# Attention and two expert layers on one core: queries held 128 tokens at a time in place of 64

## The chip, the cores and the metric

The kernel runs on one core of a Trainium2 chip. The metric is the device time of one execution in microseconds, the median over several runs. In the rows of the profile PE is the matrix engine (TensorE), PEld its weight loads, DVE the vector engine, ACT the scalar engine, POOL the GpSimd engine; SP issues most DMAs.

## What is computed

```python
# attention without softmax: 8 batches, 8 heads, 576 tokens, head size 64
kv  = np.einsum('bhsd,bhse->bhde', k, v)          # 64x64 for each batch and head
out = np.einsum('bhsd,bhde->bhse', q, kv)         # the product that is changed here
rms = np.sqrt(np.mean(out * out, axis=-1, keepdims=True) + 1e-06)
x   = out / rms * g_norm                          # then laid out as 4608 tokens x 512
# dense layer, 512 -> 768 -> 512
h = np.maximum(np.maximum(x @ w1, x @ w2), x @ w3)
x = h @ w_out
# 8 experts, 512 -> 1024 -> 512, two for each token
noisy_logits = x @ w_gate + np.log1p(np.exp(x @ w_noise)) * noise
# the two largest, a softmax over the two, and
# out[token] += weight * (relu(x @ w1[e]) @ w2[e])
```

All in fp32; the kernel gets the accuracy of the large layers with pairs of fp32r tiles (a high and a low part, three products).

## The kernel before

The 4608 tokens go through the first part in nine chunks of 512 (`NCH`, `CT`). For each chunk the kernel makes the attention output of its tokens (`ao`), norms it (`norm_a` to `norm_c`: a square on ACT, a sum for each head on DVE, a root, a scaling), turns it so that features lie on partitions (`xtrans` on TensorE in the first two chunks, `planes_out` and a transposing DMA later), multiplies it by the dense layer's 18 column groups (`g1`, L353) and back (`g2`, L399), routes the tokens (`route_a`, `route_b`) and scatters their rows to a table in DRAM. After the last chunk comes the expert stage (`unit`, with L1180, L1194 and L1242 as its matmuls), from 676 us on, which takes the larger part of the time.

`ao(c, j, banks)` makes half a chunk: two blocks `i` of 128 tokens. The keys' and values' product of a batch lies in a tile `KB` of 128 partitions x 256: two heads stand on top of each other (partitions 0 to 63 and 64 to 127, `HALF`), and the four pairs `p` of heads side by side. The queries lie in the same way, features on partitions and tokens along the row. In each call the queries are what TensorE holds (its weights) and 64 columns of `KB` what streams through. The result has tokens on partitions: head half `h` goes to bank `h`, and pair `p` and block `i` choose the columns in it. There are two banks for each half chunk, with 16 calls in each block.

A batch is 576 tokens, four and a half blocks. So at tokens 576, 1728, 2880 and 4032 the border of two batches lies in the middle of a block, and the two halves of that block need different tiles `KB`.

The order on TensorE is as the code is written, apart from the first chunk: there `run_tasks` places tasks by costs that are written beside them (`ao0`, the first half of chunk 1, is one of these, with cost 1.0, and `ao1`, the second half, is another). From chunk 2 on `attend` calls `ao` for the next chunk at the twelfth column group of `g1`, both halves one after the other, between two matmul groups of the dense layer. The tiles' results are read by the squares at once (L230), and by `norm_c` (L250) later in the same chunk.

Other matmuls in plain fp32 that are named below: L187 multiplies keys by values, with weights of 128 x 64 (two heads in two column halves) and, for the last 64 tokens of a batch, of 64 x 64; L561 is a part of the gate's weights' preparation, with weights of 128 x 128 and 16 streaming columns; L543 and L272 are transposes; L457 and L458 have 16-bit weights.

Of the kernel before, what the change touches and what calls it, by code (L numbers as in the profile page):

```python
# [18 lines left out]
NB, NH, S, D = 8, 8, 576, 64  # L19
T, DM, DF, NE, DE = 4608, 512, 768, 8, 1024  # L20
NCH, CT = 9, 512
# [61 lines left out]
def body(tc, A, dbg=None):  # L83
    nc = tc.nc
    PE, ACT, DVE, POOL, SP = nc.tensor, nc.scalar, nc.vector, nc.gpsimd, nc.sync
# [19 lines left out]
    KB = [sb1.tile([128, 256], F, name=f"kvt{i}") for i in range(2)]  # L105
# [59 lines left out]
    def qv(c):  # L165
        return qbuf[c][:, 0:2048].rearrange("p (a t) -> p a t", a=4)
# [9 lines left out]
    HALF = [slice(0, 64), slice(64, 128)]  # L176
# [25 lines left out]
    def ao(c, j, banks):  # L202
        for h in range(2):
            ao_bank[c, 2 * j + h] = banks[h]
        for i in range(2):
            t0 = (2 * j + i) * 128
            for p in range(4):
                o = slice(i * 256 + p * 64, i * 256 + (p + 1) * 64)
                for x in range(2):
                    t = t0 + x * 64  # L210
                    kb = KB[(c * CT + t) // S % 2]
                    for h in range(2):
                        PE.matmul(banks[h][HALF[x], o], qv(c)[HALF[h], p, t:t + 64],
                                  kb[HALF[h], p * 64:(p + 1) * 64], start=True, stop=True)

    xn_of = {}
    xn_n = [0]
# [98 lines left out]
    def attend(c, n):  # L316
        if n == 0:
            for j in range(2):
                ao(c, j, [abank(), abank()])
        if n < 2:  # L320
            for b in (2 * n, 2 * n + 1):
                norm_a(c, b)
        if n == 1:
            norm_b1(c, 0, 4)
            norm_b2(c, 0, 4)
        if n in (2, 3):
            j = n - 2
            for b in (2 * j, 2 * j + 1):
                norm_c(c, b)
                planes_out(c, b)  # L330
            planes_turn(c, j)
# [280 lines left out]
    for j in range(2):  # L612
        ao(0, j, [abank(), abank()])
        for i in range(2):
            norm_a(0, 2 * j + i)
# [123 lines left out]
    for i in range(2):  # L739
        if i == 0:  # L740
            task("ao0", "PE", 1.0, ["q1", "kvo", "x0l3", "ev0"] + done, lambda: ao(1, 0, [abank(), abank()]), 0)
        task(f"n1s{i}", "ACT", 0.6, ["ao0", "t03"], lambda i=i: norm_sq(1, i, x1[i]), 0.6)
        task(f"n1r{i}", "DVE", 0.69, [f"n1s{i}"], lambda i=i: norm_red(1, i), 0.6)
# [261 lines left out]
    c = NCH - 1  # L1005
# [444 lines left out]
```

## Time and profile before

| | us |
|---|---|
| median of 3 runs | 1505.43 (1503.96 to 1508.12) |
| the profiled execution | 1503.61 |
| its span in the trace | 1501.8 |
| TensorE matmuls busy | 1476.2 (98%) |
| TensorE weight loads busy | 1260.4 (84%) |
| VectorE busy | 749.5 (50%) |
| ScalarE busy | 644.2 (43%) |

The profile is of one execution. The span begins with the first recorded instruction and ends with the last; the execution's own time is 1.8 us longer. Busy time is the union of an engine's instructions; matmuls are pipelined, and a matmul's length in the rows is from its start to its modelled end, so that many can lie over each other. The same is true of weight loads: a load's length tells how long one takes, and the distance between the starts of two tells their pace.

### The profile page before, as it was taken

To read this page: it belongs to the slowest core of one execution; us is meant where nothing else is said; L and a number is where in the kernel's file an instruction comes from. 1 tells how busy PE (TensorE), PEld (TensorE's weight loads), DVE (VectorE), ACT (ScalarE), POOL (GpSimd) and SP (SyncE) were. 2 spreads that over 40 slices of the span, in tenths; PEclk is the share of its full clock that TensorE was granted. 3 is DMA by queue.
4 is the path that set the end of the run, shared out by engine and by line. 5 is a ranking of instruction groups with operands and counts; after the bars stand their busy time and mean duration, and the time that the engine had idled before them with its cause. 6 is when DMAs were issued, how large, how long until landed. Compare 5 with 4: busy or idle time off the path is not lost.

```text
span 1501.8 us, 22899 instructions
## 1 busy us (share of the span) xinstructions
PE 1476.2 (98%) x9190; PEld 1260.4 (84%) x9190; DVE 749.5 (50%) x1513; ACT 644.2 (43%) x1020; POOL 223.3 (15%) x332
## 2 busy tenths in 40 slices
PE   6999999999999999999999999999999999999997
PEld 6889989898989888888888878887888888888886
DVE  6985545454444444458344454553454374444443
ACT  4653524242424233334444454544454364444443
POOL 0000111102020202023211102202211111110112
PEclk9999999999999999999999999999999999999999
DMA  7412435142332303083776668767565587554555
GB/s 315 144 70 99 152 117 149 72 149 86 126 114 99 121 29 122 0 240 107 200 200 140 173 217 227 194 186 199 135 162 137 147 216 196 132 135 140 139 121 108
DMA packets 160724, 218.43 MB, mean 145 GB/s; under 512 B 124320, under 2 KB 124704, under 8 KB 145120
## 3 DMA queue, kind: packets, MB, share of 16 engines
q1 hardware_dynamic: 140624, 165.14, 35.0%
q0 software_dynamic: 19984, 51.73, 15.1%
q8 instruction: 74, 1.21, 0.3%
q14 instruction: 42, 0.34, 0.1%
HBM read 137.86 MB, written 51.72 MB: 126 GB/s over the span
## 4 chain that ended last, share of the span: by engine, by line
PE 54%; POOL 0%; issue 0%; ACT 0%; POOLq 0%
PE bank L1242 26%; PE bank L1180 26%; PE bank L1194 1%; PE bank L1283 1%; PE bank L1298 0%; PE bank L399 0%; POOL out L1216 0%; PE bank L1205 0%; ACT W L334 0%; PE bank L1289 0%; ACT xn L1247 0%; POOLq L1398 0%; ACT RA L406 0%; PE bank L1136 0%; POOL spacer L1215 0%
## 5 line engine op out<-in xcount | busy, mean ns | idle before, releaser
L353 PE MATMUL bank<-B,W 128*128 128x512 f32 (+1 forms) x2184 | 453.1, 367 | 2.2 <-ACT W L532 2.1
L353 PEld LDWEIGHTS bank<-B,W 128*128 128x128 f32 x2184 | 376.4, 188 | 70.4 <-ACT W L532 2.5
L1242 PE MATMUL bank<-W,B 128*128 128x512 f32 x1704 | 411.2, 390 | 0.0
L1242 PEld LDWEIGHTS bank<-W,B 128*128 128x128 f32 x1704 | 318.6, 188 | 64.5
L1180 PE MATMUL bank<-B,W 128*128 128x512 f32 (+4 forms) x1536 | 361.0, 374 | 0.0
L1180 PEld LDWEIGHTS bank<-B,W 128*128 128x128 f32 x1536 | 278.1, 188 | 53.7 <-issue 4.4
L335 DVE TENSOR_TENSOR W<-G,W 128x1024 fp32r<-128x1024 f32 x168 | 203.0, 1224 | 121.8 <-ACT W L334 121.3
L1184 ACT ACTIVATE B<-bank 128x512 fp32r<-128x512 f32 (+4 forms) x152 | 85.8, 565 | 334.3 <-PE bank L1180 334.3
L1185 DVE SCALAR_TENSOR_TENSOR B<-bank,B 128x512 fp32r<-128x512 f32 (+4 forms) x152 | 98.7, 649 | 249.0 <-ACT B L1184 248.4
L334 ACT ACTIVATE W<-G 128x1024 fp32r<-128x1024 f32 x168 | 175.4, 1055 | 43.5 <-PE bank L1242 24.9
L399 PE MATMUL bank<-W,B 128*128 128x256 f32 (+1 forms) x1296 | 161.0, 284 | 0.4 <-DVE B L361 0.2
L399 PEld LDWEIGHTS bank<-W,B 128*128 128x128 f32 x1296 | 159.5, 188 | 1.6 <-ACT RA L406 0.5
L472 POOL DMA_INDIRECT Xg<-RA,si x72 | 70.7, 981 | 582.0 <-issue 403.7
L371 DVE TENSOR_TENSOR hm<-hm,bank 128x512 f32<-128x512 f32 (+1 forms) x107 | 69.6, 651 | 115.2 <-PE bank L353 109.8
L1216 POOL DMA_INDIRECT out<-xn,idt x36 | 59.2, 1644 | 402.9 <-ACT xn L1247 397.6
L357 ACT ACTIVATE B<-hm 128x512 fp32r<-128x512 f32 (+1 forms) x53 | 32.2, 607 | 172.4 <-DVE hm L371 172.4
L1180 PE MATMUL bank<-xlo,W 128*128 128x512 f32 (+2 forms) x288 | 73.3, 376 | 0.0
L1180 PEld LDWEIGHTS bank<-xlo,W 128*128 128x128 f32 x288 | 52.5, 188 | 9.8
L369 ACT ACTIVATE hm<-bank 128x512 f32<-128x512 f32 (+1 forms) x54 | 30.4, 564 | 64.1 <-PE bank L353 52.2
L406 ACT COPY RA<-bank 128x256 uint16<-128x256 uint16 x72 | 25.6, 372 | 68.6 <-DVE RA L406 63.2
L1216 POOL DMA_INDIRECT out<-hm,idt x20 | 31.9, 1593 | 131.2 <-ACT hm L1247 127.4
L361 DVE TENSOR_TENSOR B<-hm,B 128x512 fp32r<-128x512 f32 (+1 forms) x53 | 35.1, 661 | 32.2 <-ACT B L357 32.2
(230 smaller groups left out, 1034.8 us busy)
## 6 DMA issues: line engine op xcount, KB each, us to landing
G<-mw SPq DMA_DIRECT2D x84, 1024.0 KB, 5.1
G<-w1s SPq DMA_DIRECT2D x12, 1024.0 KB, 4.9
kv<-kv SPq DMA_DIRECT2D x8, 1024.0 KB, 7.1
G<-kv SPq DMA_DIRECT2D x8, 1024.0 KB, 9.2
RB<-qT SPq DMA_DIRECT2D x8, 1024.0 KB, 4.9
G<-mw SPq DMA_DIRECT2D x16, 512.0 KB, 6.4
out<-pad POOLq DMA_DIRECT2D x5, 1280.0 KB, 6.5
out<-pad POOLq DMA_DIRECT2D x2, 1536.0 KB, 6.7
```

Source lines behind the costliest of these rows:

```text
L334: ACT.activation(w[:, 0:1024], src, AF.Copy)
L335: DVE.tensor_tensor(w[:, 1024:2048], src, w[:, 0:1024].bitcast(F), op=OP.subtract)
L353: PE.matmul(bank[:, 0:t1 - t0], w_in(g)[:, a, k, s], x[b][:, k, t0:t1], start=n == 0 and k == 0, stop=n == 2 and k == 3)
L361: DVE.tensor_tensor(h[:, 1], hm, h[:, 0].bitcast(F), op=OP.subtract)
L371: DVE.tensor_tensor(hm, hm, bank, op=OP.max)
L399: PE.matmul(x2b[i][z][:, 0:hi - lo], h[:, a, s], w[:, b, lo:hi], start=f == 0 and n == 0, stop=f == 5 and n == 2)
L472: i = POOL.indirect_dma_start(out=Xg, out_offset=bass.IndirectOffsetOnAxis(ap=idx, axis=0), in_=src, in_offset=None)
L1180: PE.matmul(bank[:, 0:n], w[:, a, k, s], x[b][:, k, 0:n], start=z == 0, stop=z == 11)
L1184: ACT.activation(h[:, 0, 0:n], bank[:, 0:n], AF.Relu)
L1185: DVE.scalar_tensor_tensor(h[:, 1, 0:n], bank[:, 0:n], 0.0, h[:, 0, 0:n].bitcast(F), op0=OP.max, op1=OP.subtract)
L1216: d = POOL.indirect_dma_start(out=A["out"], out_offset=bass.IndirectOffsetOnAxis(ap=idt[u % 3][:, i:i + 1], axis=0), in_=y, in_offset=None ...
L1242: PE.matmul(obank[i], h[:, a, s], w[:, b, ff % 2, :], start=ff == 0 and n == 0, stop=ff == 7 and n == 2)
```

## The change

A block of 128 tokens that lies in one batch is no longer cut in two. Its queries are held by TensorE as 64 x 128 tiles (64 features of a head, 128 tokens), one for each head half, where there were four of 64 x 64. A block on the border of two batches is cut as before.

```diff
             t0 = (2 * j + i) * 128
             for p in range(4):
                 o = slice(i * 256 + p * 64, i * 256 + (p + 1) * 64)
-                for x in range(2):
-                    t = t0 + x * 64
-                    kb = KB[(c * CT + t) // S % 2]
+                k = [KB[(c * CT + t) // S % 2] for t in (t0, t0 + 64)]
+                w = 128 if k[0] is k[1] else 64
+                for x in range(0, 128, w):
                     for h in range(2):
-                        PE.matmul(banks[h][HALF[x], o], qv(c)[HALF[h], p, t:t + 64],
-                                  kb[HALF[h], p * 64:(p + 1) * 64], start=True, stop=True)
+                        PE.matmul(banks[h][x:x + w, o], qv(c)[HALF[h], p, t0 + x:t0 + x + w],
+                                  k[x // 64][HALF[h], p * 64:(p + 1) * 64], start=True, stop=True)
```

TensorE's instructions where chunk 2's product begins, before the change; a row is a call, the last figures are the partitions and columns of what it writes, `bank6` and `bank7` take the two head halves, `kvt0` and `kvt1` are the two tiles `KB`, and RB has the queries:

```order
L353 MATMUL bank3_108<-B0_85,W5_75 128x256 x12
L353 MATMUL bank0_105<-B0_85,W5_75 128x256 x12
L213 MATMUL bank6_111<-kvt1_91,RB_89 64x64
L213 MATMUL bank7_112<-kvt1_91,RB_89 64x64
L213 MATMUL bank6_111<-kvt1_91,RB_89 64x64
L213 MATMUL bank7_112<-kvt1_91,RB_89 64x64
```

And the same place in the changed kernel:

```order
L353 MATMUL bank3_108<-B0_85,W5_75 128x256 x12
L353 MATMUL bank0_105<-B0_85,W5_75 128x256 x12
L213 MATMUL bank6_111<-kvt1_91,RB_89 128x64
L213 MATMUL bank7_112<-kvt1_91,RB_89 128x64
L213 MATMUL bank6_111<-kvt1_91,RB_89 128x64
L213 MATMUL bank7_112<-kvt1_91,RB_89 128x64
```

Before, the four calls are one pair of heads; in the changed kernel two calls are, and the next two are the next pair. The calls stand in the same place between the dense layer's groups.

TensorE's instructions at the border block of chunk 3 (token 1728), before the change, with the last two calls of the block ahead of it:

```order
L213 MATMUL bank6_111<-kvt0_90,RB_89 64x64
L213 MATMUL bank7_112<-kvt0_90,RB_89 64x64
L213 MATMUL bank6_111<-kvt0_90,RB_89 64x64
L213 MATMUL bank7_112<-kvt0_90,RB_89 64x64
L213 MATMUL bank6_111<-kvt1_91,RB_89 64x64
L213 MATMUL bank7_112<-kvt1_91,RB_89 64x64
```

And in the changed kernel:

```order
L213 MATMUL bank6_111<-kvt0_90,RB_89 128x64
L213 MATMUL bank7_112<-kvt0_90,RB_89 128x64
L213 MATMUL bank6_111<-kvt0_90,RB_89 64x64
L213 MATMUL bank7_112<-kvt0_90,RB_89 64x64
L213 MATMUL bank6_111<-kvt1_91,RB_89 64x64
L213 MATMUL bank7_112<-kvt1_91,RB_89 64x64
```

The border block's calls are unchanged; what is new is that their neighbours have another form. The other engines' instructions and TensorE's other ones stand in the same order in both kernels.

## Rows read from the trace of the kernel before

**Rows 1.** The page: busy us and share of the span, by engine.

```profile
PE 1476.2 (98%) x9190; PEld 1260.4 (84%) x9190; DVE 749.5 (50%) x1513; ACT 644.2 (43%) x1020; POOL 223.3 (15%) x332
```

**Rows 2.** Stretches: from and to, length, busy us by engine, granted clock, DMA.

```profile
core 0: us, PE busy (x) PEld busy (x) DVE busy (x) ACT busy (x) POOL busy (x), PEclk, DMA share, GB/s
0.00:20.00 20.00, 9.76 (x222) 8.63 (x222) 8.75 (x13) 7.71 (x13) 0.55 (x7) 1.00 0.89 350
20.00:47.00 27.00, 23.27 (x261) 19.76 (x260) 24.96 (x40) 16.74 (x26) 1.39 (x4) 1.00 0.61 240
224.00:253.00 29.00, 29.00 (x193) 26.89 (x192) 16.95 (x38) 12.86 (x24) 4.42 (x8) 1.00 0.43 102
253.00:281.00 28.00, 28.00 (x128) 23.15 (x127) 10.62 (x40) 7.52 (x13) 0.00 (x0) 1.00 0.26 107
700.00:900.00 200.00, 200.00 (x917) 164.39 (x916) 98.72 (x187) 90.59 (x133) 40.81 (x58) 1.00 0.67 187
1480.00:1501.80 21.80, 10.83 (x64) 9.24 (x62) 4.43 (x6) 4.43 (x7) 3.18 (x3) 0.86 0.36 66
```

**Rows 3.** Stretches of L213 alone: matmuls and loads, busy us and count.

```profile
113.00:115.00 2.00, 1.16 (x64) 1.02 (x64) 1.00 0.00 0
217.50:220.50 3.00, 2.10 (x128) 1.96 (x128) 1.00 0.93 348
...
sum 29.00, PE 19.21 PEld 17.83; mean PE 1.92 PEld 1.78
```

**Rows 4.** Timeline, TensorE, chunk 3's product: start, length, line, form, count.

```profile
217.76 1.96 PEld L213 LDWEIGHTS bank<-kvt,RB 64*64 64x64 f32 x128 [0.35 <-issue]
217.77 2.10 PE L213 MATMUL bank<-kvt,RB 64*64 64x64 f32 x128
...
219.79 0.53 PEld L353 LDWEIGHTS bank<-B,W 128*128 128x128 f32 x3
```

**Rows 5.** Weight loads by line and form: busy us, mean ns of one, idle before.

```profile
L353 PEld LDWEIGHTS bank<-B,W 128*128 128x128 f32 x2184 | 376.4, 188 | 70.4 <-ACT W L532 2.5 <-issue 1.2 <-DVE B L281 0.3
L213 PEld LDWEIGHTS bank<-kvt,RB 64*64 64x64 f32 x1024 | 15.8, 135 | 2.6 <-issue 2.1 <-DVE kvt L198 0.3
...
L187 PEld LDWEIGHTS bank<-kv 128*64 128x64 f32 x256 | 11.1, 148 | 8.7 <-DMA kv<-kv 8.3
...
L543 PEld LDWEIGHTS bank<-cst,RA 128*128 128x128 f32 x24 | 2.7, 144 | 0.6 <-DVE RA L528 0.4
...
L561 PEld LDWEIGHTS bank<-cst,G 128*128 128x128 f32 x12 | 1.6, 192 | 0.0
...
L458 PEld LDWEIGHTS <-trib 128*128 128x128 bf16 x9 | 0.9, 100 | 0.0
L457 PEld LDWEIGHTS <-onesb 128*128 128x128 bf16 x9 | 0.9, 96 | 2.1 <-issue 2.1
...
L552 PEld LDWEIGHTS bank<-G,wgn 128*32 128x32 f32 x24 | 0.5, 108 | 0.4
...
L1136 PEld LDWEIGHTS bank<-cst,s 128*1 128x1 f32 x2 | 0.2, 82 | 0.2
```

**Rows 6.** Timeline, TensorE's loads of L187 in the start.

```profile
28.89 0.32 PEld L187 LDWEIGHTS bank<-G 128*64 128x64 f32 x8
...
29.12 0.32 PEld L187 LDWEIGHTS bank<-kv 128*64 128x64 f32 x8
...
29.36 0.32 PEld L187 LDWEIGHTS bank<-G 128*64 128x64 f32 x8
...
29.74 0.32 PEld L187 LDWEIGHTS bank<-hm 64*64 64x64 f32 x16
```

**Rows 7.** Timeline, TensorE, one burst of L561.

```profile
101.35 0.54 PEld L561 LDWEIGHTS bank<-cst,G 128*128 128x128 f32 x4
101.47 0.52 PE L561 MATMUL bank<-cst,G 128*128 128x16 f32 x4
```

**Rows 8.** Timeline of the start: the products of chunks 0 and 1 and their readers.

```profile
15.98 1.57 ACT L230 ACTIVATE xn<-bank 128x512 f32<-128x512 f32 x3 [1.13 <-PE bank L213]
16.61 1.87 DVE L234 TENSOR_REDUCE stat<-xn 128x8 f32<-128x512 f32 x3 [1.85 <-ACT xn L230]
...
17.43 0.62 ACT L230 ACTIVATE x2T<-bank 128x512 f32<-128x512 f32 x1
...
37.31 0.69 DVE L234 TENSOR_REDUCE stat<-xn 128x8 f32<-128x512 f32 x1 [1.05 <-ACT xn L230]
...
41.67 2.11 PE L353 MATMUL bank<-B,W 128*128 128x512 f32 x8 [2.09 <-ACT W L532]
```

## The prediction, made before the changed kernel had run

> **What bounds the kernel now.** I read the engine totals first: TensorE is busy for 1476.2 of 1501.8 us, the next engine for 749.5 [rows 1]. The totals mix stages, so the table of stretches came second. From the second chunk on, TensorE is busy in all of every stretch (29.00 of 29, 28.00 of 28, 200.00 of 200), at a granted clock of 1.00. Only the start (9.76 of the first 20 us, 23.27 of the next 27) and the last 22 us have idle time [rows 2]. So whatever the attention product takes longer or shorter on TensorE comes out in the end time one for one, except perhaps in the start.
>
> Third, the product's own line. A chunk's 128 matmul instructions (64 calls, each two instructions, each with a weight load) take 2.10 us where the chunk is whole, 1.16 us for a half; nine chunks make 19.2 us in all [rows 3]. That is the most that this change could ever win. The next TensorE line's first load begins 2.03 us after the product's first (219.79 against 217.76) [rows 4], so the chunk pays 2.03 us, and nothing fills it from elsewhere.
>
> Fourth, what sets that pace. The 128 loads last 1.96 us from first start to last end, one load 135 ns [rows 4, 5]. Four tiles take turns, 32 loads each, so the loads of one tile follow each other by (1960 - 135) / 31 = 59 ns. The product of keys and values (L187) has two tiles side by side instead of four, and its groups of eight loads start 0.235 us apart (28.89, 29.12, 29.36 us) [rows 6]: four loads for each tile, again 59 ns. So the pace belongs to the tile, not to the number of instructions. And it goes with the tile's weight columns: one load takes 82 ns with 1 column, 108 with 32, 135 with 64, 188 to 192 with 128, while 128 rows in place of 64 change 135 to 148 at most [rows 5].
>
> **What is removed and added.** Of 36 blocks of 128 tokens, batches of 576 tokens cut four (at 576, 1728, 2880 and 4032); these keep their 16 calls of 64x64. The other 32 go from 16 calls to 8: 576 calls become 320, and 1152 matmul instructions 640. Seen from one tile nothing gets fewer. A 64x64 tile has 4 calls in a block (one for each pair of heads), so 8 loads and 8 matmuls; a 64x128 tile, of which there are only two, also has 4 calls, 8 loads and 8 matmuls of the same 64 columns. What changes is that each load now brings 128 columns.
>
> The price of that. Two rows give it. By duration a load of 128 columns takes 188 (L353) to 192 (L561) against 135 ns: 53 to 57 ns more [rows 5]. By pace, the four loads of L561, whose matmuls have only 16 columns and so cannot be what they wait for, last 0.54 us together at 192 ns each: (540 - 192) / 3 = 116 ns apart, 57 more than 59 [rows 7]. I take 55, the middle, since both ends are 128-column rows. It is paid 8 times in a block, if the two row halves load side by side as the four quadrants do now: 8 x 55 = 0.44 us, a chunk's product going from 2.0 to about 3.8 us. Over 32 blocks 256 x 55 ns = **14.1 us** (13.6 to 14.6).
>
> Changes of form. In chunks 1, 3, 5 and 7 the product now passes between 64x128 and 64x64 tiles 1 + 2 + 2 + 1 = 6 times. The trace has no such passage; the nearest is L187 going from 128x64 to 64x64, where 0.38 us lie between the starts (29.36 to 29.74) in place of 0.235 [rows 6]. Bounds 0 and 0.145 us each; I take the row: 6 x 0.145 = **0.9 us**. Entering and leaving the stage was a change of form before and stays one.
>
> What could hide it. In the first chunk the squares on ACT wait for the product (idle 1.13 us to 15.98), the reductions on DVE for the squares (1.85), and the transposes on TensorE for those [rows 8]. ACT now starts the third square as it ends the second; it would wait for the second pair of banks until about 18.6 us, and its last square end some 1.8 us later. Nothing catches this up, as DVE is busy for 24.96 of the next 27 us [rows 2]; it is paid in full, as counted. In chunk 1 the first half lies in a stretch where TensorE waits 2.09 us for ACT at 41.67, but DVE at 37.31 waits for this product's square too (1.05), and ACT's conversions come out of DVE's work [rows 8]; at most 0.44 + 0.15 = 0.6 us is hidden there, and I count 0. The other engines' instructions are the same in the same order; no DMA, bank or wait is added. The banks' first readers come 1.8 us later in a chunk, and TensorE needs their results only in the next window, so nothing queues up behind. The expert stage from 676 us on only starts later.
>
> Sum: 14.1 + 0.9 = 15.0 us on the profiled execution's 1503.61, so 1518.6. The median of the runs is 1505.43, 1.8 above that execution; shifted by the same 15.0 I forecast **1520** us.
>
> **Rivals.** *The wide load is hidden* (no change). 128-column loads are not always long here: those of the transposes (L543) take 144 ns, those of 16-bit weights (L457, L458) 96 and 100 [rows 5]. If the 64x128 load were of that kind, it would stay near or under the 59 ns that a 64-column tile needs now, and each chunk would take its 2.0 us as before: 1505.4, or 1506.3 with the changes of form. Against it: the operands are plain fp32 as in L561 (192 ns), and nothing is transposed. A rule speaks for a part of this: the Trainium skill, in TensorEngine Tiling (Array Packing), section Restrictions, says that tiling by columns switches fast weight loading off, and the new form has no column tiling. By that rule alone the sum would be 0; but TensorE: Matmul & The Clock Gate, section "Weight-path perf modes — Fast Weight Load (FWL) and DoubleRow", excludes fp32 from it, and the trace agrees with the exclusion (192 ns in fp32, 96 in 16 bit).
>
> *TensorE is paced by instructions* (faster). Four loads of the quadrants go out in 59 ns, one every 14.4 ns (1825 / 127). Were it the sending and not the loading that filled this time, 512 fewer instructions would give back 7.4 us: 1498. It decides from the point where two wide tiles are done within 29 ns. L187 speaks against it: half as many instructions in the same time per tile [rows 6]. The skill's TensorEngine Tiling page, section Instruction Overhead, puts some 60 cycles on every matmul however few its columns, which is the rule behind such a gain; no row here shows a load of 128 fp32 columns as short as that.
>
> *Load and matmul do not overlap in a wide tile* (slower still). A matmul of 64 columns adds about 53 ns to 116, if it costs what its 64-column load costs beyond 82 ns; 110 ns more per load than now: 28 us and 0.9, so 1534. The totals speak against it: matmuls of 1476.2 us and loads of 1260.4 us, nearly all of 128 columns, share one span of 1501.8 us [rows 1]. *The two row halves load one after the other*: 16 loads of 116 ns in a block, 1.86 in place of 0.47 us, 32 x 1.39 = 44 us: 1550. Against it: 14.4 ns between loads of different quadrants, two of them in each row half.
>
> **Chances and range.** Forecast 0.80; hidden load 0.09; instruction pace 0.03; no overlap 0.05; one after the other 0.03. The forecast's own range: 53 and no cost of form and 0.6 hidden give 13.0, 57 and the full cost 15.5, so 1518 to 1521; the runs before spread from 1503.96 to 1508.12, and the 55 ns come from tiles of another shape, whose first 64 columns could hide a few ns more or less. At 30 ns for a wide load the sum is 7.7, at 80 it is 21.4: 1513 to 1527 holds what I believe of the forecast, and leaves the rivals outside, 0.2 together. A change under 0.3% (4.5 us) cannot be told from none here: faster 0.03, same 0.09, slower 0.88.
>
> **What would show it.** Right: L213 with 512 matmuls of 64x128 and 128 of 64x64, loads of 188 to 192 ns, a whole chunk's product about 3.8 us long, and the chunks' stretches longer by 1.5 to 1.8 us each, with TensorE still without idle time. Wrong: loads near 140 ns and 2.0 us per chunk (hidden); under 1.5 us (instruction pace); 5 us or more (no overlap). If the products grow as forecast and the end does not, a wait in the chunks took it up, and rows 2 misled me. If chunks with a border block grow more than those without, the changes of form cost far more than 0.145 us.

## The result, and the profile after

The changed kernel takes 1520.32 us (median of 6 runs, 1517.25 to 1522.76) against 1505.30 (6 runs, 1502.46 to 1508.12): the ratio is 1.0097, 95% interval 1.0080 to 1.0114. The forecast was 1520, from 15 us more. The profiled execution of the changed kernel took 1522.76 us, 2.4 above the median, and that surplus leads to the place where the forecast's working was off. No execution took 1520 us: three lie at 1517.25 to 1518.39 and three at 1522.24 to 1522.76, and the median is the middle between the two groups.

The totals first. Matmuls are busy for 20 us more and loads for 19 us more, the other engines as before [rows 1]:

```profile
PE 1496.5 (98%) x8678; PEld 1279.4 (84%) x8678; DVE 750.7 (49%) x1513; ACT 645.2 (42%) x1020; POOL 222.8 (15%) x332
```

The stretches that answer to [rows 2] show TensorE without a gap after the start, as before; so what it does longer, the kernel does longer:

```profile
core 0: us, PE busy (x) PEld busy (x) DVE busy (x) ACT busy (x) POOL busy (x), PEclk, DMA share, GB/s
0.00:20.00 20.00, 10.07 (x131) 9.58 (x131) 7.10 (x9) 6.12 (x8) 0.54 (x7) 1.00 0.89 349
20.00:47.00 27.00, 25.64 (x247) 21.68 (x245) 20.73 (x34) 13.87 (x25) 0.93 (x4) 1.00 0.51 201
231.00:260.00 29.00, 29.00 (x181) 26.30 (x180) 15.37 (x34) 12.58 (x23) 4.50 (x8) 1.00 0.36 108
```

The product's stretches, against [rows 3]: chunk 2 (from 160 us, all blocks wide), chunk 3 (from 226, one border block) and chunk 7 (from 518, one border block at its end):

```profile
160.00:165.00 5.00, 3.79 (x64) 3.65 (x64) 1.00 0.11 42
226.00:231.00 5.00, 3.67 (x80) 3.39 (x80) 1.00 0.95 356
...
518.00:523.00 5.00, 3.52 (x80) 3.31 (x80) 1.00 0.83 319
```

A whole chunk's product lasts 3.79 us in place of 2.10, with half the instructions. Its loads by form, against [rows 5] (in the first of these rows 64 loads of the first chunk raise the mean):

```profile
L213 PEld LDWEIGHTS bank<-kvt,RB 64*128 64x128 f32 x464 | 30.1, 207 | 2.7 <-issue 2.1 <-DVE kvt L198 0.3
L213 PEld LDWEIGHTS bank<-kvt,kv 64*128 64x128 f32 x48 | 2.8, 187 | 0.1
L213 PEld LDWEIGHTS bank<-kvt,RB 64*64 64x64 f32 x96 | 1.7, 134 | 0.2
```

A 64x128 load takes 187 ns, as the 128x128 loads do, where a 64x64 load takes 134. Of two tiles each has 32 of the 64 loads, so they follow each other by (3650 - 187) / 31 = 112 ns, where it was 59: the two row halves do load side by side.

The timeline of the loads gives the price of a chunk, since TensorE never waits between two products (start, length):

```profile
160.99 3.65 PEld L213 LDWEIGHTS bank<-kvt,RB 64*128 64x128 f32 x64
...
226.44 3.53 PEld L213 LDWEIGHTS bank<-kvt,RB 64*128 64x128 f32 x80 [0.35 <-issue]
...
299.48 3.65 PEld L213 LDWEIGHTS bank<-kvt,RB 64*128 64x128 f32 x64 [0.35 <-issue]
```

The first and the last of these starts in the kernel before (the middle one, 217.76 us, is in [rows 4]):

```profile
154.00 1.96 PEld L213 LDWEIGHTS bank<-kvt,RB 64*64 64x64 f32 x128
...
289.24 1.96 PEld L213 LDWEIGHTS bank<-kvt,RB 64*64 64x64 f32 x128 [0.35 <-issue]
```

From chunk 2's product to chunk 3's it is 65.45 us, before 63.76: a chunk with four wide blocks costs 1.69 us, 0.42 for each block. From chunk 3's to chunk 4's it is 73.04, before 71.48: 1.56 with three wide blocks and two changes of form, so a change costs (1.56 - 3 x 0.42) / 2 = 0.15 us.

The first chunk is another matter. In the kernel before, its product and the matmuls that follow it (L576, the same 14 in both kernels) took 2.19 and 3.45 us:

```profile
14.68 2.19 PE L213 MATMUL bank<-kvt,RB 64*64 64x64 f32 x128 [0.21 <-DVE kvt L198]
...
16.80 3.45 PE L576 MATMUL bank<-cst 128*128 128x270 f32 x14
```

In the changed kernel they took 7.29 and 5.94 us:

```profile
14.52 7.29 PE L213 MATMUL bank<-kvt,RB 64*128 64x64 f32 x64
18.23 1.09 ACT L230 ACTIVATE xn<-bank 128x512 f32<-128x512 f32 x2 [3.45 <-PE bank L213]
...
21.64 0.60 ACT L230 ACTIVATE xn<-bank 128x512 f32<-128x512 f32 x1 [2.33 <-PE bank L213]
...
21.73 5.94 PE L576 MATMUL bank<-cst 128*128 128x270 f32 x14
```

A single load of the product there takes up to 335 ns:

```profile
L213 PEld LDWEIGHTS bank<-kvt,RB x560: 129/188/335, 14.5 to 592.7; 64*128 64x128 f32 x155, 64*64 64x64 f32 x32
```

These are 1.7 to 1.8 times the durations elsewhere (188 ns, 3.45 us), which speaks for the lower of TensorE's two levels, 1.2 in place of 2.4 GHz. The table of stretches says 1.00 for the granted clock here, but the clock's record in the trace has no entry ahead of 26.8 us, where full speed begins. In the profile of before it begins at 14.2 us, just ahead of the product. The second chunk's product then begins 5.7 us later; first the kernel before, then the changed one:

```profile
35.47 1.16 PE L213 MATMUL bank<-kvt,kv 64*64 64x64 f32 x64
```

```profile
41.14 1.73 PE L213 MATMUL bank<-kvt,kv 64*64 64x64 f32 x48
```

So one of two things was true: the wide product goes with a late rise, or this execution had one by chance.

### The profile page after: what moved, and what is told of

It is laid out like the page before. It is cut to its first block, busy times and chain, and to the rows that moved or that the text cites. A ratio compares the mean times of both kernels' runs of the same rounds, so it can differ in the third digit from the quotient of the medians.

```text
span 1521.0 us, 21872 instructions
## 1 busy us (share of the span) xinstructions
PE 1496.5 (98%) x8678; PEld 1279.4 (84%) x8678; DVE 750.7 (49%) x1513; ACT 645.2 (42%) x1020; POOL 222.8 (15%) x332
## 4 chain that ended last, share of the span: by engine, by line
PE 97%; DVE 1%; DMA 1%; ACT 0%; POOL 0%; issue 0%; SPq 0%; POOLq 0%; DVEq 0%
PE bank L353 29%; PE bank L1242 26%; PE bank L1180 25%; PE bank L399 10%; PE bank L213 2%; PE bank L187 1%; PE bank L1194 1%; DMA G<-kv 1%; PE bank L1283 0%; PE bank L1298 0%; PE bank L576 0%; POOL out L1216 0%; PE bank L543 0%; PE bank L272 0%; ACT W L532 0%
## 5 line engine op out<-in xcount | busy, mean ns | idle before, releaser
L1180 PE MATMUL bank<-B,W 128*128 128x512 f32 (+4 forms) x1536 | 361.2, 374 | 0.0
L1180 PEld LDWEIGHTS bank<-B,W 128*128 128x128 f32 x1536 | 278.0, 188 | 54.0 <-issue 4.4
L1180 PE MATMUL bank<-xlo,W 128*128 128x512 f32 (+2 forms) x288 | 73.3, 376 | 0.0
L1180 PEld LDWEIGHTS bank<-xlo,W 128*128 128x128 f32 x288 | 52.5, 188 | 9.8
```

Source lines behind the costliest of these rows:

```text
L1180: PE.matmul(bank[:, 0:n], w[:, a, k, s], x[b][:, k, 0:n], start=z == 0, stop=z == 11)
```

## The experiments

Each run stands against runs of the kernel before on the same chip. The kernel before itself took 1510.40 us in the first group of runs, 1506.44 and 1506.20 in the others. Times are therefore compared within a group.

### More streamed columns in the wide tiles

Is it the load that a wide tile waits for, or the stream? Each call now streams its own pair's columns and the next lower pair's, which a later call writes over.

```diff
-            for p in range(4):
-                o = slice(i * 256 + p * 64, i * 256 + (p + 1) * 64)
+            for p in (3, 2, 1, 0):
+                s = slice(max(p - 1, 0) * 64, (p + 1) * 64)
+                o = slice(i * 256 + s.start, i * 256 + s.stop)
...
-                                  k[x // 64][HALF[h], p * 64:(p + 1) * 64], start=True, stop=True)
+                                  k[x // 64][HALF[h], s], start=True, stop=True)
```

> The changed kernel, but each call streams 128 columns of KB where it can (its own pair of heads and the next lower one, whose part is written over by the next call; the last call of a block keeps 64), so 3 of 4 calls stream twice the columns and the loads stay as they are. Load theory (a tile is held up by the longer of its weight load and its stream, some 107 ns for 128 weight columns): 128 streamed columns take as long as the load, nothing or a few ns are added; a whole chunk's product 3.8 to 4.0 us as in the changed kernel (3.79), and 1520 to 1522 us. Rival, stream (the wide tile is slow because its stream is, 110 ns for 64 columns): 6 of a tile's 8 passes in a block grow by about 110 ns, 32 x 0.66 = 21 us: 1541, a whole chunk's product 6.4 us.

1526.59 us (1524.04 to 1530.04), ratio 1.0104 (1.0087 to 1.0121) to its own group's before. The whole chunk's product, on the timeline:

```profile
304.84 3.79 PE L214 MATMUL bank<-kvt,RB 64*128 64x128 f32 x64
```

It is 3.79 us, to the last digit the changed kernel's, with 1.75 times the columns streamed. The stream of 64 columns lay wholly beside the load, and a stream of 128 still does. The rival is out. (The time expected was reckoned from a kernel before of 1505; the 16 us above before hold the border blocks' narrow tiles too, which the doubling does slow.)

### More streamed columns in the narrow tiles

The same edit of `p`, `s` and `o` in the kernel before, with its calls of 64 tokens.

> The kernel before, with the same doubling of streamed columns in 64x64 tiles; loads stay at 64 columns. Load theory: load (53 ns) and stream (about 53 ns for 64 columns) lie beside each other, so doubling the stream alone makes it the longer of the two, about 107 ns: 6 of a tile's 8 passes grow by some 50 ns, 0.3 us for each of 36 blocks, 10.8 us: 1516, a whole chunk's product 3.3 us. Rival, loads alone set the pace and a stream of 64 columns takes far less: 59 ns stay, 1505 and 2.1 us. Rival, load and stream follow one another (27 + 27): 6 x 27 x 36 = 5.8 us: 1511 and 2.7 us.

1522.82 us (1521.42 to 1525.79), ratio 1.0092 (1.0075 to 1.0108). A whole chunk's product:

```profile
300.38 3.32 PE L214 MATMUL bank<-kvt,RB 64*64 64x128 f32 x128
```

3.32 us, where 3.3 was expected for load and stream side by side. So in a 64x64 tile load and stream are nearly equally long, and making either of them longer costs about the same: 1.22 us over the 24 doubled passes of a tile are 51 ns for each, and the wide load's were 53. Of the 12.4 us over before (10.8 were expected), 9 x 1.22 = 11.0 are the longer streams. In the profiled execution two products took longer than that, 5.24 us in chunk 2 and 4.30 us in chunk 8, with TensorE standing still for 0.25 to 0.54 us at a time, waiting for nothing that the profile shows; why is open.

### The head halves one after the other

```diff
-            for p in range(4):
-                ...
-                for x in range(0, 128, w):
-                    for h in range(2):
+            for h in range(2):
+                for p in range(4):
+                    ...
+                    for x in range(0, 128, w):
```

> The changed kernel with the loops over head halves and pairs swapped in each block: first the four calls of one row half, then the four of the other, so neighbours in the queue are on the same wide tile; the same work otherwise, border blocks too. If TensorE takes loads far out of order, the two halves still load side by side: 1520, a chunk's product 3.8 us. If it only looks a call or so ahead, 16 loads of a block follow one another with an overlap at the turn of halves: about 0.8 us more for each of 32 wide blocks and some 0.2 to 0.4 for the four border blocks, 26 us: 1546, and a product of about 7 us. My theory of the result does not depend on which; I expect the second more (0.65).

1536.80 us (1536.33 to 1537.65), ratio 1.0178 (1.0161 to 1.0195): 26 us above before, 11 more than the change itself. A whole chunk:

```profile
309.95 4.61 PE L213 MATMUL bank<-kvt,RB 64*128 64x64 f32 x64
```

4.61 us is neither of the two that I had expected. A block takes (4.61 - 3.79) / 4 = 0.2 us more than with alternating halves, a quarter of what loads strictly one behind the other were expected to cost. The loads' start times in the trace show how: the first five are 0.11 us apart, the pace of one tile alone; from then on until the last few they are 0.05 to 0.06 us apart, the pace of two tiles together, but for one step of 0.11 us in every eight. So TensorE finds most of the work for the other half although it stands eight matmuls further back in the queue, but not all; how far it looks was not measured. A chunk with a border block pays more, 5.04 us where the change took 3.67:

```profile
235.51 5.04 PE L213 MATMUL bank<-kvt,RB 64*128 64x64 f32 x80
```

Added up over the chunks, the products are 9.5 us longer than in the changed kernel's profile, of the 11.

### Every second block

```diff
-                w = 128 if k[0] is k[1] else 64
+                w = 128 if k[0] is k[1] and i == 1 else 64
```

> The changed kernel with wide tiles only in every second block (i = 1): 16 wide blocks in place of 32, and 23 changes of form inside the products in place of 6. Load theory with the cost of form as in the forecast: 16 x 0.42 = 6.8 us and 23 x 0.147 = 3.4 us, 10.2 us in all: 1515.5, a whole chunk's product 2.10 + 0.85 + 0.44 = 3.4 us. If changes of form cost nothing: 6.8 us, 1512, 2.95 us. Rival, a fixed cost for each chunk that has wide tiles at all (a change of mode, not the loads): as the changed kernel, 1520, 3.8 us.

1522.55 us (1519.62 to 1523.78), ratio 1.0086 (1.0069 to 1.0103), 12.2 us above before against 10.2 expected; the interval's lower end is 10.4, and where the other 2 us lie is open. The products of a whole chunk and of chunk 3, which has one wide block and one change of form:

```profile
226.73 2.67 PE L213 MATMUL bank<-kvt,RB 64*64 64x64 f32 x112
```

```profile
298.77 3.40 PE L213 MATMUL bank<-kvt,RB 64*64 64x64 f32 x96
```

3.40 us was the number expected with a cost of form, against 2.95 without, and 2.67 is 2.10 + 0.42 + 0.15. Here 16 wide blocks fewer save 16 x 0.42 = 6.7 us, and 17 more changes of form take 2.6 of it back. (The rows name one form; they merge both.)

### The first chunk

Four kernels were run in one group and two in another: the change again, the change with chunk 0 narrow, both kernels with early matmuls, chunk 0 alone wide, and the kernel before again.

> The changed kernel as it is, as the measure for the other runs of this group. In its first profile chunk 0's product took 7.29 us in place of 2.19, and the record of the granted clock begins at full speed only behind it. If that belongs to the change: product of chunk 0 about 7 us again, and 14 to 19 us above the kernel before. If it was a chance of that execution: 3.8 us in chunk 0 here, as in the later whole chunks, and 13 to 16 us above.

1521.46 us (1517.08 to 1525.63), ratio 1.0094 (1.0069 to 1.0120). Its first product again took 7.29 us:

```profile
14.67 7.29 PE L213 MATMUL bank<-kvt,RB 64*128 64x64 f32 x64
```

and again the clock's record begins late, at 27.0 us. The profiled execution is this kernel's slowest, 1525.63. What it takes longer than the first profile lies behind the chunks, whose last product begins at 589.44 us (first profile: 589.22); from 692.6 to 695.9 us the granted clock is 0.50 there. So not all of the spread between executions comes from the start.

```diff
-                w = 128 if k[0] is k[1] else 64
+                w = 128 if k[0] is k[1] and c > 0 else 64
```

> The changed kernel with 64x64 tiles kept in chunk 0 alone. Load theory: chunks 1 to 8 keep their cost (about 12 us by the starts of the products), chunk 0 takes 2.2 us; 1.7 us under the changed kernel where the clock is at 2.4 GHz by then, 3.5 to 5 us under it where it is still at 1.2. Rival, the start hides the first product (the engines wait for weights there anyway): the same time as the changed kernel.

1517.75 us (1516.75 to 1521.11), ratio 1.0087 (1.0065 to 1.0108). Its two products of the start:

```profile
14.63 2.29 PE L213 MATMUL bank<-kvt,RB 64*64 64x64 f32 x128
...
35.50 1.73 PE L213 MATMUL bank<-kvt,kv 64*64 64x64 f32 x48
```

The second begins at 35.50 us, as in the kernel before (35.47); in the profile of the changed kernel it begins at 41.14. So the start hides what the first product takes longer at most in part. With chunk 0 out of the way, this profiled execution (1516.75) is 13.1 us above that of before. The median is 3.7 us under the change again, as expected for a late rise, but with four executions of each the intervals overlap. Chunk 8's product begins 11.06 us later than in the kernel before, whose row is the first:

```profile
572.60 2.12 PE L213 MATMUL bank<-kvt,RB 64*64 64x64 f32 x128
```

```profile
583.66 3.79 PE L213 MATMUL bank<-kvt,RB 64*128 64x64 f32 x64
```

For the next two, 56 matmuls were put ahead of the first product of keys and values:

```diff
     first = [abank() for p in range(4)]
+    for _ in range(56):
+        PE.matmul(HB[3][:, 0:128], ones, ones, start=True, stop=True)
     kv_all(0, first)
```

> The kernel before, with 56 matmuls of 16-bit ones ahead of the first product of keys and values, while TensorE has nothing to do (0.9 to 7 us). If the late rise of the clock costs the start time in some executions: the clock is at 2.4 GHz from some 5 us on, chunk 0's product 2.1 us in each execution, and 0 to 3 us less than before. If the clock falls again in the waits for the first loads (8 to 13 us): no difference.

1508.09 us (1506.43 to 1508.77), ratio 1.0012 (1.0002 to 1.0021): no gain, rather 1.7 us lost. The stretches show why the early rise does not last. The granted clock was at full speed from 6.6 us on, and it was at half again from 10.0 us, behind two microseconds in which TensorE had been busy for 0.45; later it fell once more, behind three with 0.91 us of work:

```profile
8.00:10.00 2.00, 0.45 (x8) 0.31 (x8) 1.89 (x2) 0.94 (x1) 0.00 (x0) 1.00 0.99 416
10.00:13.40 3.40, 2.76 (x52) 2.76 (x54) 1.65 (x2) 1.06 (x1) 0.00 (x0) 0.51 1.01 413
...
41.00:44.00 3.00, 0.91 (x5) 0.49 (x4) 2.76 (x7) 2.65 (x6) 0.00 (x0) 1.00 0.22 38
44.20:47.50 3.30, 3.30 (x12) 2.66 (x11) 3.09 (x4) 0.21 (x2) 0.00 (x0) 0.50 0.66 278
```

The second fall does not come from the early matmuls: the kernel before, profiled again (the last run below), has one at the same place.

```profile
43.20:46.50 3.30, 3.30 (x13) 2.70 (x12) 2.88 (x3) 0.40 (x1) 0.00 (x0) 0.50 0.65 271
```

By the product the clock was up again, but the product then stood still for 2.1 us in its midst, waiting for nothing that the profile shows (the row's "issue"):

```profile
14.34 1.60 PE L213 MATMUL bank<-kvt,RB 64*64 64x64 f32 x87 [0.20 <-DVE kvt L198]
18.05 0.85 PE L213 MATMUL bank<-kvt,RB 64*64 64x64 f32 x41 [2.11 <-issue]
```

What this stall is stays open.

> The changed kernel with the same early matmuls. If chunk 0's 7.29 us were the clock: 3.8 us here, and 3 to 5 us less than the changed kernel in the executions that had a late rise; against the kernel before with early matmuls 14 to 15 us more, the forecast's sum. If the wide tiles are slow in chunk 0 for another reason (the queries' or keys' data come late): 7 us again, no gain.

1520.33 us (1517.91 to 1523.61), ratio 1.0104 (1.0081 to 1.0127). In the profiled execution, the fastest of the four, the clock was up from 14.4 us, and the wide product of chunk 0 took 3.98 us:

```profile
14.42 3.98 PE L213 MATMUL bank<-kvt,RB 64*128 64x64 f32 x64
```

This profile also shows what the clock does to a known instruction. From 11.0 to 14.4 us its record has half speed, and L187's loads last 227 ns in it:

```profile
L187 PEld LDWEIGHTS bank<-G 128*64 128x64 f32 x24 | 1.7, 227 | 0.0
```

In the kernel before the same loads last 138 ns at full speed (27 to 31 us, first row), and in the first profile of the changed kernel 224 ns from 8 to 14 us, where there is no record (second row):

```profile
L187 PEld LDWEIGHTS bank<-G 128*64 128x64 f32 x32 | 1.3, 138 | 0.0
```

```profile
L187 PEld LDWEIGHTS bank<-G 128*64 128x64 f32 x32 | 2.2, 224 | 2.0 <-DMA G<-kv 2.0
```

So TensorE did run at 1.2 GHz ahead of the record's first entry, and the 7.29 us were the clock and not the queries or keys. But the executions still spread over 5.7 us, and the median is 1.1 us under the change without early matmuls, well inside the interval. The slower an execution, the lower its mean granted clock (0.997, 0.996, 0.994, 0.992): the slower ones were longer at half speed, and no trace of them shows where. Against the kernel before with early matmuls it is 12.2 us more, where 14 to 15 were expected; that kernel's stall of 2.1 us would make up the difference, if every execution has it, which was not seen.

```diff
-                w = 128 if k[0] is k[1] else 64
+                w = 128 if k[0] is k[1] and c == 0 else 64
```

> The kernel before with 64x128 tiles in chunk 0 alone: what the change costs in the start by itself. Theory, load and clock: if the clock's record begins late again (20 to 27 us), chunk 0's product takes about 7 us and chunk 1's first product begins at about 41 us (before: 35.5), 5 to 6 us above the kernel before; in executions with an early rise 4 us and some 1 us above. So the times spread over two groups, 1 and 5 us above the kernel before. Rival, the late rise in three profiles was chance: a rise at 14 to 15 us, product of 3.8 to 4 us, 1 to 2 us above the kernel before in every execution.

1506.44 us (10 runs, 1505.16 to 1510.94), ratio 1.0010 (0.9999 to 1.0021): the first chunk's part is 1.5 us by the ratio, which compares means, with an interval from 0 to 3.2; the medians differ by 0.2. The two groups that were expected are not clear: two of the ten executions lie 3.5 and 4.7 us above the median of before, the others at most 2.1. The profile had an early rise, at 14.0 us, and shows

```profile
14.55 3.89 PE L213 MATMUL bank<-kvt,RB 64*128 64x64 f32 x64 [0.21 <-DVE kvt L198]
...
36.67 1.16 PE L213 MATMUL bank<-kvt,kv 64*64 64x64 f32 x64
```

chunk 1 beginning 1.2 us later than before. The first product is 1.70 us longer than before's 2.19, so about 0.5 us of it is hidden. A wide first product does not bring a late rise with it each time.

> The kernel before, profiled a second time. By the theory that wide tiles in chunk 0 go with the late rise of the clock: rise at 14 to 15 us and a product of 2.1 to 2.3 us again. By the rival of chance: a rise as late as 20 to 27 us can come here too, with a product of about 4 us.

1507.63 us in its one execution. The rise came at 15.8 us, inside the product, which took 2.69 us. So the rise varies in the kernel before too. Over all profiles without early matmuls it came at 14.2, 14.4, 15.1, 14.6 and 15.8 us where the first chunk was narrow or half narrow, and at 26.8, 27.0, 26.2, 19.7 and 14.0 us where it was wide. Late rises were seen with wide tiles only, in four profiles of five; why, no run here tells.

## Why the prediction was right, and where it was off

**The bound.** TensorE without gaps from the second chunk on: right; the sums of the products came out in the end time. The expert stage's first load (L1180) begins 19.0 us later in the changed profile (694.9 against 675.9), so nearly all of the loss lies ahead of it, as forecast:

```profile
L1180 PEld LDWEIGHTS bank<-B,W x1536: 186/188/192, 675.9 to 1486.3; 128*128 128x128 f32 x192
```

```profile
L1180 PEld LDWEIGHTS bank<-B,W x1536: 186/188/192, 694.9 to 1505.6; 128*128 128x128 f32 x192
```

**The price of a wide load.** Forecast 55 ns more, between 53 and 57. Measured 112 - 59 = 53, the lower end, which came from the loads' lengths; the pace read from L561 was too high by 4 ns. For a block 0.42 us and not 0.44, over 28 blocks in chunks 1 to 8 11.8 us in place of 12.3. That the load is what counts is shown, not only argued: 1.75 times the streamed columns cost a wide tile nothing and lengthened a narrow tile's product from 2.10 to 3.32 us. (The range's two ends were not taken alike: 7.7 us at 30 ns leaves the changes of form out, 21.4 at 80 ns has them in.)

**The changes of form.** 0.145 us from one pair of rows of another line; 0.15 measured, and the kernel with 23 of them bears it out.

**Chunks 1 to 8 together.** 28 x 0.42 + 6 x 0.15 = 12.7 us. From the profile with chunk 0 narrow: its products go from level with before to 11.06 us behind at chunk 8's start (583.66 against 572.60), and 1.7 for chunk 8's own make 12.8.

**The first chunk.** This is the step that was off. It was "paid in full, as counted", 1.8 us. With the clock up, it is 1.2 us. With the clock at 1.2 GHz, as in the two profiles of the changed kernel, chunk 1 begins 5.7 and 5.8 us later. I had put the granted clock at 1.00 from the table of stretches for the start too. The profile of before did hold a warning: loads of L187 last 138 ns at the median and up to 232, and all the long ones lie in the first 14.1 us.

```profile
L187 PEld LDWEIGHTS bank<-G x352: 129/138/232, 10.7 to 497.8; 128*64 128x64 f32 x128, 64*64 64x64 f32 x48
```

That the median met the forecast to a third of a microsecond was therefore luck. 12.7 us and 1.2 or 5.7 make 13.9 or 18.4; the six executions lie in two groups, on average 12.6 and 17.2 us above the median of before, each 1.2 to 1.3 under such a sum, and 15.0 lies between them. The 4.6 us between the groups is close to the 4.5 us between an early and a late rise. That this is what parts them is likely and not shown, since one of the six was profiled, and the expectation of two such groups did not come out clearly with chunk 0 alone wide.

**The rivals.** Hidden load: out, by the length of 187 ns. Pace by instructions: out; half the instructions took 1.8 times as long (3.79 us against 2.10). No overlap of load and stream: out, by the doubled stream. The halves one after the other: out; and even the queue's order that invites it reaches only a quarter of the way.

None of these versions beats the kernel before, and none pointed to one that would: in 64x64 tiles load and stream are nearly in balance at 59 ns.

## What to carry to other kernels

With plain fp32 operands and 64 streamed columns, what TensorE paid here is the number of weight columns that each tile has to take in, one tile beside the other, and not the number of instructions: four 64x64 tiles took in the same weights in 59 ns that two 64x128 tiles took in in 112. Before tiles are merged to save instructions, compare the load's length with the stream's; only the longer one counts. And work at a kernel's start is priced at the clock of that moment, so read the length of a known instruction there: the clock's column said 1.00 while the loads took 1.6 to 1.8 times as long.

## What had not been expected of the hardware

- Load and stream of a tile overlap so well that a whole chunk's product came out at 3.79 us with 64 and with mostly 128 streamed columns over 128 weight columns.
- A change between 64x64 and 64x128 tiles costs 0.15 us of TensorE's time.
- Of two row halves queued eight matmuls apart, TensorE still overlaps most loads (4.61 us for a chunk; 3.79 with alternating halves).
- TensorE's clock stayed at 1.2 GHz through 12 us without a gap of the wide product and the matmuls behind it (14.5 to 26.8 us), in two profiles of the same kernel, and was up by 14 to 16 us in others.
- Where the clock's record has no entry yet, the table shows 1.00 although TensorE runs at half speed: the loads of L187 took 224 ns there, 227 where the record says 0.50 and 138 at full speed.
